# Attention and gated feed-forward on one core: a prologue with its weight casts, dummy matmuls and exps moved to other places and engines

## The chip, the cores and the metric

The kernel runs on one core of one Trainium2 chip. The time is the device time of one execution in microseconds (us); lower is better. The span in the profile is about 1.8 us shorter than that time. The granted clock is the share of full speed that the records show for TensorE; here it is 1.0 or 0.5, and its mean over the span is given. Five engines work side by side, each through its own queue of instructions in the order of the program: TensorE (PE in the profile), VectorE (DVE), ScalarE (ACT), GpSimd (POOL) and SyncE (SP), which here issues all DMAs.

## The reference, cut to what matters

```python
# attention, per batch b (8) and head h (8); seq 576, head_dim 64
q_s = softmax(q, axis=-1)                  # over head_dim
k_s = softmax(k, axis=2)                   # over the sequence
kv  = einsum('bhsd,bhse->bhde', k_s, v)
x   = einsum('bhsd,bhde->bhse', q_s, kv)   # -> [4608 tokens, 512]
# feed-forward
h   = (x @ w1) * (x @ w2) @ w3             # w1, w2: 512x1024, w3: 1024x1024
out = h @ w_out                            # 1024x512
```

Inputs and the output are float32. The kernel casts to float16 on the chip and computes `W3O = w3 @ w_out` once, so that the feed-forward is two large steps: `s1` (both products with x, multiplied) and `s2` (times `W3O`).

## The kernel before

There are nine chunks of 512 tokens. Chunk j runs eight groups of `s1(j)` with the four groups of `s2(j-1)` between them, the attention "pieces" of batch j+1 and the elementwise work of batch j+2. This steady part comes after a prologue: attention of batch 0, `s1(0)`, the product `W3O`, `s2(0)`, attention of batch 1. The order in which the source issues instructions is the order in each engine's queue (`manual_schedule`).

```python
    def norm_q(b, i, eng):                 # eng is always nc.gpsimd (POOL)
        nc.vector.reciprocal(...)
        eng.tensor_tensor(out=eqn, in0=eqs, in1=dr, op=ALU.mult)
    ...
    def w3_t(ft):                          # cast a row block of w3, transpose it
        w316 = attn.tile([P, Fd], F16, tag="w316", name="w316", bufs=2)
        nc.gpsimd.tensor_copy(out=w316, in_=w32[("3", ft)])      # POOL
        ... eight transposes on PE, then a copy on DVE (w3T)
    def w3_m(ft):
        ... eight matmuls w3T x wosb, then nc.scalar.copy(out=W3O[ft], in_=wps)
    ...
    for fb in range(N_FT):
        s1(0, fb)
        ...
        if fb == 5:
            w3_t(0)
            for i in range(4):
                pcopy(out=wosb[i], in_=w32[("o", i)])            # POOL
        if fb == 6:
            w3_t(1)
    ...
    def elementwise_steps(b): ...          # ten steps: exp_q, sum_q, norm_q, exp_k, cast_v
    ew = elementwise_steps(1)
    for ft in range(N_FT):
        w3_m(ft)
        if ft + 2 < N_FT:
            w3_t(ft + 2)
        if ft == 4:
            ew[0](); ew[1](); ew[2]()      # ew[2] holds norm_q(1, 0): POOL
        if ft == 5: ...
    pc = pieces(1)
    s2(0, 0); pc[0](); s2(0, 1, alt=True); pc[1](); ...          # pieces of batch 1
    for f in elementwise_steps(2):         # all of batch 2's exps in one burst
        f()
    for j in range(1, N_CHUNK): ...        # pieces at steps 0, 1, 3, 5, 7 of twelve
```

`warm(n)` issues n dummy matmuls on a zero tile, to keep TensorE's clock up while real work waits.

The softmax here doesn't subtract the row's maximum and nothing guards it: scores larger than these inputs give would overflow.

Of the kernel before, what the change touches and what calls it, by code (L numbers as in the profile page):

```python
# [8 lines left out]
F32 = mybir.dt.float32  # L9
F16 = mybir.dt.float16  # L10
# [6 lines left out]
def kernel(  # L17
# [11 lines left out]
    nc = tc.nc  # L29
# [3 lines left out]
    P = 128  # L33
# [25 lines left out]
    def pAtt(shape, dtype):  # L59
        return psum.tile(shape, dtype, tag="att", name="att", bufs=2)  # L60

    def pAB():
        return psum.tile([P, CH], F32, tag="pab", name="pab", bufs=3)
# [10 lines left out]
    def load_qkv(b, which, i):  # L74
        src = {"q": q, "k": k, "v": v}[which]
        t = slot([P, 2, R * D])
        nc.sync.dma_start(  # L77
            out=t,
            in_=src[b, 4 * i:4 * i + 4].rearrange("(h g) (s r) d -> (g s) h (r d)", g=2, r=R))
        qkv32[(which, b, i)] = t  # L80
# [16 lines left out]
    def load_w3(ft):  # L97
        t = slot([P, Fd])
        nc.sync.dma_start(out=t, in_=moe_w3[ft * P:(ft + 1) * P, :])
        w32[("3", ft)] = t  # L100
# [4 lines left out]
    def exp_k(b, i, hh):  # L105
        if hh == 0:
            eks[(b, i)] = attn.tile([P, R, 2, D], F16, tag="ek", name="ek", bufs=4)
        nc.scalar.activation(  # L108
            out=eks[(b, i)][:, :, hh, :],
            in_=qkv32[("k", b, i)][:, hh].rearrange("p (r d) -> p r d", r=R), func=AF.Exp)  # L110
# [8 lines left out]
    def cast_v(b, i, copy, hhs=slice(0, 2)):  # L119
        copy(out=v16buf[b % 2][:, 2 * i:2 * i + 2, :, 0:D][:, hhs],  # L120
             in_=qkv32[("v", b, i)].rearrange("p h (r d) -> p h r d", r=R)[:, hhs])
# [21 lines left out]
    def piece_kv(b, i):  # L143
        kvp = pAtt([P, 2, 512], F32)
        for r in range(R):
            for g in range(2):
                rows = slice(64 * g, 64 * g + 64)
                nc.tensor.matmul(kvp[:, g, 0:130].rearrange("p (h e) -> p h e", h=2),  # L148
                                 lhsT=eks[(b, i)][rows, r].rearrange("p h d -> p (h d)"),
                                 rhs=v16buf[b % 2][rows, 2 * i:2 * i + 2, r, 0:65],  # L150
                                 start=(r == 0), stop=(r == R - 1))
        rc = attn.tile([P, 2], F32, tag="rc", name="rc", bufs=4)
        nc.vector.reciprocal(out=rc, in_=kvp[:, :, 64])
        kv2 = attn.tile([P, 2, D], F16, tag="kv2", name="kv2", bufs=4)
        for hh in range(2):
            sl = slice(64 * hh, 64 * hh + 64)
            nc.vector.tensor_tensor(
                out=kv2[sl], in0=kvp[sl, :, 65 * hh:65 * hh + 64],
                in1=rc[sl, :, None].broadcast_to([64, 2, 64]), op=ALU.mult)
        kvs[(b, i)] = kv2  # L160

    def piece_t(b, i):
        pt = pAtt([P, R, P], F16)
        for r in range(R):
            nc.tensor.transpose(pt[:, r, :], eqns[(b, i)][:, r].rearrange("p h d -> p (h d)"),  # L165
                                ident)
        qsT = attn.tile([P, 2, R, SP], F16, tag="qsT", name="qsT", bufs=3)
        nc.vector.tensor_copy(out=qsT.rearrange("p g r s -> p r g s"),  # L168
                              in_=pt.rearrange("p r (g s) -> p r g s", g=2))
        qsTs[(b, i)] = qsT.rearrange("p g r s -> p g (r s)")  # L170

    def piece_x(b, i, hf):
        xp = pAtt([P, 2, 512], F32)
        qsT, kv2 = qsTs[(b, i)], kvs[(b, i)]
        cols = slice(hf * HS, (hf + 1) * HS)
        for hh in range(2):
            rows = slice(64 * hh, 64 * hh + 64)
            for g in range(2):
                nc.tensor.matmul(xp[64 * g:64 * g + 64, hh, 0:HS], lhsT=kv2[rows, g, :],  # L179
                                 rhs=qsT[rows, g, cols], start=True, stop=True)  # L180
        nc.scalar.copy(out=xT[:, 2 * i:2 * i + 2, b * S + hf * HS:b * S + (hf + 1) * HS],  # L181
                       in_=xp[:, :, 0:HS])

    def pieces(b):
        return {0: lambda: piece_t(b, 0), 1: lambda: piece_t(b, 1),
                3: lambda: (piece_kv(b, 0), piece_kv(b, 1)),
                5: lambda: (piece_x(b, 0, 0), piece_x(b, 0, 1)),
                7: lambda: (piece_x(b, 1, 0), piece_x(b, 1, 1))}

    def warm(n):  # L190
        wp = pAtt([P, CH], F32)
        for _ in range(n):
            nc.tensor.matmul(wp, lhsT=zero[:, 0:P], rhs=zero, start=True, stop=True)

# [33 lines left out]

    w3Ts = {}

    def w3_t(ft):
        w316 = attn.tile([P, Fd], F16, tag="w316", name="w316", bufs=2)
        nc.gpsimd.tensor_copy(out=w316, in_=w32[("3", ft)])
        tp = pAtt([P, N_FT, P], F16)
        for gt in range(N_FT):
            nc.tensor.transpose(tp[:, gt, :], w316[:, gt * P:(gt + 1) * P], ident)  # L236
        w3T = attn.tile([P, N_FT, P], F16, tag="w3T", name="w3T", bufs=2)
        nc.vector.tensor_copy(out=w3T, in_=tp)  # L238
        w3Ts[ft] = w3T

    def w3_m(ft):
        wps = pO() if ft % 2 else pAB()
        for gt in range(N_FT):
            nc.tensor.matmul(wps, lhsT=w3Ts[ft][:, gt, :], rhs=wosb[gt // 2][:, gt % 2, :],  # L244
                             start=(gt == 0), stop=(gt == N_FT - 1))
        nc.scalar.copy(out=W3O[ft], in_=wps)
# [17 lines left out]
    for t in v16buf:  # L264
        nc.gpsimd.memset(t[:, :, :, 64:65], 1.0 / SC)

    warm(18)
    for i in range(2):
        for hh in range(2):
            exp_q(0, i, hh)  # L270
# [9 lines left out]
        load_wo(i)  # L280
    piece_t(0, 0)
    cast_v(0, 0, vcopy)
    warm(4)
    piece_t(0, 1)
    piece_kv(0, 0)
    exp_k(0, 1, 0)
    exp_k(0, 1, 1)
    cast_v(0, 1, acopy, slice(1, 2))
    piece_x(0, 0, 0)
    piece_x(0, 0, 1)  # L290
    cast_v(0, 1, vcopy, slice(0, 1))
    piece_kv(0, 1)
    vcopy(out=w1sb[0], in_=w32[(0, 0)])
    acopy(out=w2sb[0], in_=w32[(1, 0)])
    piece_x(0, 1, 0)
    piece_x(0, 1, 1)

    def cast_w12(qt):
        vcopy(out=w1sb[qt], in_=w32[(0, qt)])
        acopy(out=w2sb[qt], in_=w32[(1, qt)])  # L300

    for fb in range(N_FT):
        s1(0, fb)
        if fb == 0:
            cast_w12(1)
        if fb == 2:
            cast_w12(2)
        if fb == 4:
            cast_w12(3)
        if fb == 5:  # L310
            w3_t(0)
            for i in range(4):
                pcopy(out=wosb[i], in_=w32[("o", i)])
        if fb == 6:
            w3_t(1)
    for ft in range(2, 8):
        load_w3(ft)
    for which, i in LOADS:
        load_qkv(1, which, i)
    for which, i in LOADS:  # L320
        load_qkv(2, which, i)

    def elementwise_steps(b):
        st = []
        for i in range(2):
            st += [lambda i=i: exp_q(b, i, 0),
                   lambda i=i: (sum_q(b, i, 0), exp_q(b, i, 1)),
                   lambda i=i: (sum_q(b, i, 1), norm_q(b, i, nc.gpsimd))]
        for i in range(2):
            st += [lambda i=i: exp_k(b, i, 0),  # L330
                   lambda i=i: (cast_v(b, i, pcopy), exp_k(b, i, 1))]
        return st

    ew = elementwise_steps(1)
    for ft in range(N_FT):
        w3_m(ft)
        if ft + 2 < N_FT:
            w3_t(ft + 2)
        if ft == 4:
            ew[0]()  # L340
            ew[1]()
            ew[2]()
        if ft == 5:
            ew[3]()
            ew[4]()
            ew[5]()
        if ft == 6:
            ew[6]()
            ew[7]()
        if ft == 7:  # L350
            ew[8]()
            ew[9]()
    pc = pieces(1)
    s2(0, 0)
    pc[0]()
    s2(0, 1, alt=True)
    pc[1]()
    s2(0, 2)
    pc[3]()
    s2(0, 3, alt=True)  # L360
    pc[5]()
    pc[7]()
    for which, i in LOADS:
        load_qkv(3, which, i)
    for f in elementwise_steps(2):
        f()

    seq = [("g", 0), ("g", 1), ("t", 0), ("g", 2), ("g", 3), ("t", 1),
           ("g", 4), ("g", 5), ("t", 2), ("g", 6), ("g", 7), ("t", 3)]
    for j in range(1, N_CHUNK):  # L370
        pc = pieces(j + 1) if j + 1 < B else {}
        ew = elementwise_steps(j + 2) if j + 2 < B else []
        ld = LOADS if j + 3 < B else []
        for n, (kind, x) in enumerate(seq):
            if kind == "g":
                s1(j, x)
            elif j > 1:
                s2(j - 1, x)
            if n in pc:
                pc[n]()  # L380
            if n < len(ew):
                ew[n]()
            if n >= 4 and n - 4 < len(ld):
                load_qkv(j + 3, *ld[n - 4])
    for tb in range(4):
        s2(N_CHUNK - 1, tb, alt=tb % 2)

# [29 lines left out]
```

## Time and profile before

| | before |
|---|---|
| time, median of 2 runs | 272.95 us |
| span of the profiled run | 271.1 us |
| PE busy | 246.7 us (91%) |
| mean granted clock of TensorE | 0.969 |
| first `s1` matmul of chunk 1, of chunk 2 | 74.5 us, 97.3 us |

The rows below are from the page of the kernel before: the span in 40 slices of 6.8 us, each digit the busy share in tenths. PEclk is the granted TensorE clock in tenths, DMA the busy share of the DMA engines.

```profile
PE   8579779669749999999999999999999999999983
PEclk9968979979998999999999999999999999999999
DMA  7999999941399903593498359411311113212235
```

From the thirteenth slice on (81 us) PE is full. All that can be won cheaply lies in the first twelve slices. DMA is full from the start to about 59 us: that is the reading of inputs and weights.

The timeline of PE in the kernel before, three of its lines: start, duration, operation, count, and in brackets how long PE sat idle before it and what ended that.

```profile
35.55 0.90 PE L236 MATMUL att<-ident,w_416 128*128 128x128 f16 x8 [3.17 <-POOL w_416 L233]
56.32 1.03 PE L236 MATMUL att<-ident,w_614 128*128 128x128 f16 x8 [4.15 <-POOL w_614 L233]
80.02 1.09 PE L165 MATMUL att<-ident,eqn 128*128 128x128 f16 x9 [3.21 <-POOL eqn L134]
```

PE waits three times for POOL by more than 3 us (two waits of 2.09 and 0.54 us in the first 12 us are left out): for the cast of w3 piece 1 (`w_416`), of w3 piece 7 (`w_614`), and for a normalised q of batch 2 (`eqn`). The timeline of POOL in the kernel before shows why the first two casts are late (the columns are the same):

```profile
26.77 1.04 POOL L233 CAST w_385<-st 128x1024 f16<-128x1024 f32 x1 [15.54 <-DMA st<-in_moe_w_dram]
29.43 1.35 POOL L313 CAST wo_83<-st 128x1024 f16<-128x1024 f32 x1 [1.63 <-DMA st<-in_moe_w_out_dram]
...
33.47 1.04 POOL L313 CAST wo_86<-st 128x1024 f16<-128x1024 f32 x1 [0.30 <-DMA st<-in_moe_w_out_dram]
34.45 1.04 POOL L233 CAST w_416<-st 128x1024 f16<-128x1024 f32 x1
...
53.16 2.12 POOL L134 TENSOR_TENSOR eqn<-eq,dr 128x1152 f16<-128x1152 f16 x1 [5.90 <-DMA st<-in_q_dram]
55.23 1.04 POOL L233 CAST w_614<-st 128x1024 f16<-128x1024 f32 x1
```

By the landing records of the trace, `w_416` landed at 28.02 us, before all of w_out (29.38 to 33.41), but is cast after it: POOL's queue holds four w_out casts first, and each of them starts within 0.1 us of its landing. `w_614` landed at 41.12 us and stands behind `eqn`. POOL had nothing to do from 47.3 to 53.2 us: it is not busy, it is blocked. (The trace puts the 5.90 us down to a DMA of q. The q piece of batch 1 had landed by 42.6 us; its exp started on ACT only at 50.5 us, behind the `W3O` copy of the same loop step, and the sum and reciprocal on DVE ended at 53.0 us.)

The table by windows for the kernel before, with windows laid on the stretches in which its clock records show half speed, and one of the steady part; the value after the engines is the granted clock:

```profile
15.25:22.08 6.83, 5.98 (x24) 1.92 (x21) 2.46 (x6) 3.65 (x5) 0.00 (x0) 0.50 1.09 348
35.73:39.14 3.41, 3.41 (x15) 1.57 (x13) 0.69 (x1) 0.58 (x1) 1.79 (x2) 0.50 1.03 408
56.21:59.62 3.41, 3.30 (x14) 1.74 (x15) 2.13 (x4) 0.00 (x0) 0.05 (x1) 0.50 0.33 122
80.10:83.52 3.42, 3.42 (x16) 1.77 (x17) 1.45 (x2) 1.50 (x4) 3.42 (x3) 0.50 1.05 402
100.00:150.00 50.00, 50.00 (x350) 24.20 (x349) 29.69 (x55) 24.35 (x42) 12.83 (x8) 1.00 0.61 185
```

After each of the three gaps TensorE runs at half clock for 3.41 us: about 1.7 us more is lost (an estimate, half of 3.41). A fourth stretch, 15-22 us, follows the thin attention work of batch 0.

### The profile page before, as it was taken

To read this page: it belongs to the slowest core of one execution; us is meant where nothing else is said; L and a number is where in the kernel's file an instruction comes from. 1 tells how busy PE (TensorE), PEld (TensorE's weight loads), DVE (VectorE), ACT (ScalarE), POOL (GpSimd) and SP (SyncE) were. 2 spreads that over 40 slices of the span, in tenths; PEclk is the share of its full clock that TensorE was granted. 3 is DMA by queue.
4 is the path that set the end of the run, shared out by engine and by line. 5 is a ranking of instruction groups with operands and counts; after the bars stand their busy time and mean duration, and the time that the engine had idled before them with its cause. 6 is when DMAs were issued, how large, how long until landed. Compare 5 with 4: busy or idle time off the path is not lost.

```text
span 271.1 us, 4141 instructions
## 1 busy us (share of the span) xinstructions
PE 246.7 (91%) x1574; PEld 116.7 (43%) x1574; DVE 132.3 (49%) x235; ACT 108.0 (40%) x182; POOL 62.8 (23%) x50
## 2 busy tenths in 40 slices
PE   8579779669749999999999999999999999999983
PEld 3234335334325455445444544544454444444431
DVE  2735523433466648636734863673553344444432
ACT  5464302514293773543473355347214322212200
POOL 1600654144055623410360342036000000000000
PEclk9968979979998999999999999999999999999999
DMA  7999999941399903593498359411311113212235
GB/s 250 383 348 377 396 404 394 390 178 38 89 290 393 386 11 104 145 335 98 126 293 263 80 135 323 143 41 39 77 41 39 39 41 73 45 39 63 55 76 117
DMA packets 25300, 48.51 MB, mean 179 GB/s; under 512 B 2240, under 2 KB 6336, under 8 KB 25280
## 3 DMA queue, kind: packets, MB, share of 16 engines
q1 hardware_dynamic: 25280, 48.24, 56.0%
q8 instruction: 12, 0.20, 0.3%
q14 instruction: 8, 0.07, 0.1%
HBM read 38.80 MB, written 9.44 MB: 178 GB/s over the span
## 4 chain that ended last, share of the span: by engine, by line
PE 72%; DMA 16%; ACT 3%; POOL 2%; DVE 2%; SPq 1%; issue 1%; POOLq 0%; DVEq 0%
PE po L220 21%; PE pab L203 21%; PE pab L209 20%; DMA st<-in_moe_w_dram 8%; DMA st<-in_q_dram 4%; DMA st<-in_moe_w_out_dram 4%; PE att L165 3%; PE att L220 3%; PE att L148 3%; PE att L179 2%; POOL eqn L134 2%; PE pab L244 1%; ACT xT L181 1%; DVE osb L223 1%; SPq L77 1%
## 5 line engine op out<-in xcount | busy, mean ns | idle before, releaser
L134 POOL TENSOR_TENSOR eqn<-eq,dr 128x1152 f16<-128x1152 f16 x16 | 33.9, 2121 | 100.3 <-DVE dr L132 87.3
L220 PEld LDWEIGHTS <-abT 128*128 128x128 f16 x288 | 27.4, 98 | 34.4 <-issue 3.1
L223 DVE TENSOR_SCALAR osb<-po 128x512 f32<-128x512 f32 x32 | 22.1, 692 | 32.0 <-PE po L220 31.4
L181 ACT CAST xT<-att 128x576 f16<-128x576 f32 x32 | 18.9, 642 | 21.6 <-PE att L179 21.6
L127 DVE TENSOR_REDUCE ds<-eq 128x9 f32<-128x576 f16 x32 | 23.1, 742 | 6.8 <-ACT eq L115 6.8
L115 ACT ACTIVATE eq<-st 128x576 f16<-128x576 f32 x32 | 21.2, 686 | 2.6 <-DMA st<-in_q_dram 2.6
L108 ACT ACTIVATE ek<-st 128x576 f16<-128x576 f32 x32 | 20.7, 686 | 3.1 <-DMA st<-in_k_dram 3.1
L203 PE MATMUL pab<-xT,w_0_75 128*128 128x512 f16 x72 | 21.2, 417 | 0.5 <-ACT xT L181 0.5
L209 PE MATMUL pab<-xT,w_0_79 128*128 128x512 f16 x72 | 19.8, 400 | 0.0
L203 PE MATMUL pab<-xT,w_3_78 128*128 128x512 f16 x72 | 19.4, 393 | 0.0
L209 PE MATMUL pab<-xT,w_3_82 128*128 128x512 f16 x72 | 19.1, 388 | 0.1
L203 PE MATMUL pab<-xT,w_2_77 128*128 128x512 f16 x72 | 18.5, 380 | 0.0
L203 PE MATMUL pab<-xT,w_1_76 128*128 128x512 f16 x72 | 18.5, 380 | 0.0
L209 PE MATMUL pab<-xT,w_2_81 128*128 128x512 f16 x72 | 18.5, 379 | 0.0
L209 PE MATMUL pab<-xT,w_1_80 128*128 128x512 f16 x72 | 18.5, 379 | 0.0
L165 PE MATMUL att<-ident,eqn 128*128 128x128 f16 x144 | 11.1, 224 | 5.8 <-POOL eqn L134 5.8
L165 PEld LDWEIGHTS <-eqn 128*128 128x128 f16 x144 | 9.5, 100 | 10.4 <-POOL eqn L134 7.3
L220 PE MATMUL po<-W3O_87,abT 128*128 128x512 f16 x32 | 12.2, 381 | 1.5 <-DVE osb L223 0.8
L238 DVE COPY w3T<-att 128x1024 f16<-128x1024 f16 x8 | 5.5, 690 | 15.0 <-PE att L236 15.0
L168 DVE COPY qsT<-att 128x1152 f16<-128x1152 f16 x16 | 12.0, 749 | 1.7 <-PE att L165 1.6
L220 PE MATMUL po<-W3O_91,abT 128*128 128x512 f16 x32 | 12.1, 379 | 0.0
L220 PE MATMUL po<-W3O_92,abT 128*128 128x512 f16 x32 | 12.1, 379 | 0.0
(288 smaller groups left out, 361.3 us busy)
## 6 DMA issues: line engine op xcount, KB each, us to landing
st<-in_q_dram SPq DMA_DIRECT2D x16, 576.0 KB, 5.1
st<-in_k_dram SPq DMA_DIRECT2D x16, 576.0 KB, 7.6
st<-in_v_dram SPq DMA_DIRECT2D x16, 576.0 KB, 7.6
out_dram<-osb SPq DMA_DIRECT2D x72, 128.0 KB, 2.4
st<-in_moe_w_dram SPq DMA_DIRECT2D x16, 512.0 KB, 10.4
st<-in_moe_w_out_dram SPq DMA_DIRECT2D x4, 512.0 KB, 10.9
```

Source lines behind the costliest of these rows:

```text
L108: nc.scalar.activation(out=eks[(b, i)][:, :, hh, :], in_=qkv32[("k", b, i)][:, hh].rearrange("p (r d) -> p r d", r=R), func=AF.Exp)
L115: nc.scalar.activation(out=eqs[(b, i)][:, :, hh, :], in_=qkv32[("q", b, i)][:, hh].rearrange("p (r d) -> p r d", r=R), func=AF.Exp)
L127: nc.vector.tensor_reduce(out=dss[(b, i)][:, :, hh], in_=eqs[(b, i)][:, :, hh, :], axis=AX.X, op=ALU.add)
L134: eng.tensor_tensor(out=eqn.rearrange("p r h d -> p (r h) d"), in0=eqs[(b, i)].rearrange("p r h d -> p (r h) d"), in1=dr[:, :, None].broad ...
L148: nc.tensor.matmul(kvp[:, g, 0:130].rearrange("p (h e) -> p h e", h=2), lhsT=eks[(b, i)][rows, r].rearrange("p h d -> p (h d)"), rhs=v16bu ...
L165: nc.tensor.transpose(pt[:, r, :], eqns[(b, i)][:, r].rearrange("p h d -> p (h d)"), ident)
L168: nc.vector.tensor_copy(out=qsT.rearrange("p g r s -> p r g s"), in_=pt.rearrange("p r (g s) -> p r g s", g=2))
L181: nc.scalar.copy(out=xT[:, 2 * i:2 * i + 2, b * S + hf * HS:b * S + (hf + 1) * HS], in_=xp[:, :, 0:HS])
L203: nc.tensor.matmul(pa, lhsT=w1sb[qt][:, ct, fo:fo + P], rhs=xT[:, ct, t0:t0 + CH], start=(ct == 0), stop=(ct == N_CT - 1))
L209: nc.tensor.matmul(pb, lhsT=w2sb[qt][:, ct, fo:fo + P], rhs=xT[:, ct, t0:t0 + CH], start=(ct == 0), stop=(ct == N_CT - 1))
L220: nc.tensor.matmul(po, lhsT=abT[(j, ft)][:, tb * P:(tb + 1) * P], rhs=W3O[ft], start=(ft == 0), stop=(ft == N_FT - 1))
L223: nc.vector.tensor_scalar(out=osb, in0=po, scalar1=ISC, scalar2=None, op0=ALU.mult)
```

## The change

Its intent: no cast on an engine that is blocked, casts in the order in which weights arrive, no cold clock, and the exps of batch 2 not in one burst. The core of the diff:

```diff
-        nc.scalar.copy(out=xT[...], in_=xp[:, :, 0:HS])
+        (copy or nc.scalar.copy)(out=xT[...], in_=xp[:, :, 0:HS])   # DVE for one of batch 0's copies
 ...
     def warm(n):
-        wp = pAtt([P, CH], F32)
+        wp = pAB()
 ...                                  # dummies: 18, 4 (22)  ->  26, 6, 3, 3, 2 (40)
+    def w3_c(ft):
+        w316s[ft] = attn.tile([P, Fd], F16, tag="w316", name="w316", bufs=3)
+        (nc.scalar.copy if ft % 2 else nc.vector.tensor_copy)(out=w316s[ft], in_=w32[("3", ft)])
     def w3_t(ft):
-        w316 = attn.tile([P, Fd], F16, tag="w316", name="w316", bufs=2)
-        nc.gpsimd.tensor_copy(out=w316, in_=w32[("3", ft)])
+        w316 = w316s[ft]
 ...
         if fb == 5:
+            w3_c(0)
+        if fb == 6:
+            w3_c(1)
             w3_t(0)
-            for i in range(4):
-                pcopy(out=wosb[i], in_=w32[("o", i)])
-        if fb == 6:
-            w3_t(1)
+            vcopy(out=wosb[0], in_=w32[("o", 0)])
+            vcopy(out=wosb[1], in_=w32[("o", 1)])
+    w3_t(1)
+    vcopy(out=wosb[2], in_=w32[("o", 2)])
+    vcopy(out=wosb[3], in_=w32[("o", 3)])
+    w3_c(2)
 ...                                  # in the loop over ft:
         w3_m(ft)
+        if ft + 3 < N_FT:
+            w3_c(ft + 3)
         if ft + 2 < N_FT:
             w3_t(ft + 2)
 ...                                  # exps of batch 2 between the groups of s2(0):
     s2(0, 1, alt=True)
-    pc[1]()
+    ew[0]()
+    ew[1]()
+    pc[2]()
+    ew[2]()
     s2(0, 2)
 ...
-    for f in elementwise_steps(2):
-        f()
 ...                                  # chunk 1: pieces of batch 2, exps of batch 3
-            if n in pc:
+        pcs = dict(zip((3, 4, 6, 8, 10) if j == 1 else (0, 1, 3, 5, 7), pieces(j + 1) ...))
+            ews.setdefault(min(n + 3, 11) if j == 1 else n, []).append(f)
```

The loads of w3 and of batches 1 and 2 are also written earlier in the source, but their order on SP's queue is the same. Not shown either: the exps of batch 1 are dealt out differently over the w3 loop, batch 1's first piece stands before `s2(0, 0)`, and in the steady part each load is issued one step later.

More of the change, by code (lines that the diff above doesn't have):

```diff
@@ L170, in piece_t, with piece_x @@
         qsTs[(b, i)] = qsT.rearrange("p g r s -> p g (r s)")
-    def piece_x(b, i, hf):
+    def piece_x(b, i, hf, copy=None):
         xp = pAtt([P, 2, 512], F32)
@@ L180, in piece_x @@
                                  rhs=qsT[rows, g, cols], start=True, stop=True)
-        nc.scalar.copy(out=xT[:, 2 * i:2 * i + 2, b * S + hf * HS:b * S + (hf + 1) * HS],
-                       in_=xp[:, :, 0:HS])
+        (copy or nc.scalar.copy)(
+            out=xT[:, 2 * i:2 * i + 2, b * S + hf * HS:b * S + (hf + 1) * HS],
+            in_=xp[:, :, 0:HS])
     def pieces(b):
-        return {0: lambda: piece_t(b, 0), 1: lambda: piece_t(b, 1),
-                3: lambda: (piece_kv(b, 0), piece_kv(b, 1)),
-                5: lambda: (piece_x(b, 0, 0), piece_x(b, 0, 1)),
-                7: lambda: (piece_x(b, 1, 0), piece_x(b, 1, 1))}
+        return [lambda: piece_t(b, 0), lambda: piece_t(b, 1),
+                lambda: (piece_kv(b, 0), piece_kv(b, 1)),
+                lambda: (piece_x(b, 0, 0), piece_x(b, 0, 1)),
+                lambda: (piece_x(b, 1, 0), piece_x(b, 1, 1))]
     def warm(n):
-        wp = pAtt([P, CH], F32)
+        wp = pAB()
         for _ in range(n):
@@ L229 @@
     w3Ts = {}
+    w316s = {}
+    def w3_c(ft):
+        w316s[ft] = attn.tile([P, Fd], F16, tag="w316", name="w316", bufs=3)
+        (nc.scalar.copy if ft % 2 else nc.vector.tensor_copy)(out=w316s[ft], in_=w32[("3", ft)])
     def w3_t(ft):
-        w316 = attn.tile([P, Fd], F16, tag="w316", name="w316", bufs=2)
-        nc.gpsimd.tensor_copy(out=w316, in_=w32[("3", ft)])
+        w316 = w316s[ft]
         tp = pAtt([P, N_FT, P], F16)
@@ L265 @@
         nc.gpsimd.memset(t[:, :, :, 64:65], 1.0 / SC)
-    warm(18)
+    warm(26)
     for i in range(2):
@@ L282 @@
     cast_v(0, 0, vcopy)
-    warm(4)
+    warm(6)
     piece_t(0, 1)
     piece_kv(0, 0)
+    warm(3)
     exp_k(0, 1, 0)
@@ L291 @@
     cast_v(0, 1, vcopy, slice(0, 1))
+    warm(3)
     piece_kv(0, 1)
+    warm(2)
     vcopy(out=w1sb[0], in_=w32[(0, 0)])
@@ L295 @@
     piece_x(0, 1, 0)
-    piece_x(0, 1, 1)
+    piece_x(0, 1, 1, vcopy)
     def cast_w12(qt):
@@ L300, in cast_w12 @@
         acopy(out=w2sb[qt], in_=w32[(1, qt)])
+    for ft in range(2, 8):
+        load_w3(ft)
+    for which, i in LOADS:
+        load_qkv(1, which, i)
+    for which, i in LOADS:
+        load_qkv(2, which, i)
     for fb in range(N_FT):
@@ L310 @@
         if fb == 5:
+            w3_c(0)
+        if fb == 6:
+            w3_c(1)
             w3_t(0)
-            for i in range(4):
-                pcopy(out=wosb[i], in_=w32[("o", i)])
-        if fb == 6:
-            w3_t(1)
-    for ft in range(2, 8):
-        load_w3(ft)
-    for which, i in LOADS:
-        load_qkv(1, which, i)
-    for which, i in LOADS:
-        load_qkv(2, which, i)
+            vcopy(out=wosb[0], in_=w32[("o", 0)])
[4 more added lines that the diff above has]
+    w3_c(2)
     def elementwise_steps(b):
@@ L334 @@
     ew = elementwise_steps(1)
+    pc = pieces(1)
     for ft in range(N_FT):
         w3_m(ft)
+        if ft + 3 < N_FT:
+            w3_c(ft + 3)
         if ft + 2 < N_FT:
             w3_t(ft + 2)
-        if ft == 4:
-            ew[0]()
-            ew[1]()
-            ew[2]()
-        if ft == 5:
-            ew[3]()
-            ew[4]()
-            ew[5]()
-        if ft == 6:
-            ew[6]()
-            ew[7]()
-        if ft == 7:
-            ew[8]()
-            ew[9]()
-    pc = pieces(1)
+        for f in {4: ew[0:2], 5: ew[2:5], 6: ew[5:8], 7: ew[8:9]}.get(ft, []):
+            f()
+    pc[0]()
+    ew[9]()
+    ew = elementwise_steps(2)
     s2(0, 0)
-    pc[0]()
+    pc[1]()
     s2(0, 1, alt=True)
-    pc[1]()
+    ew[0]()
+    ew[1]()
+    pc[2]()
+    ew[2]()
     s2(0, 2)
+    ew[3]()
     pc[3]()
+    ew[4]()
     s2(0, 3, alt=True)
-    pc[5]()
-    pc[7]()
+    pc[4]()
+    ew[5]()
+    ew[6]()
+    ew[7]()
     for which, i in LOADS:
         load_qkv(3, which, i)
-    for f in elementwise_steps(2):
-        f()
     seq = [("g", 0), ("g", 1), ("t", 0), ("g", 2), ("g", 3), ("t", 1),
@@ L370 @@
     for j in range(1, N_CHUNK):
-        pc = pieces(j + 1) if j + 1 < B else {}
-        ew = elementwise_steps(j + 2) if j + 2 < B else []
+        pcs = dict(zip((3, 4, 6, 8, 10) if j == 1 else (0, 1, 3, 5, 7),
+                       pieces(j + 1) if j + 1 < B else []))
+        steps = elementwise_steps(j + 2) if j + 2 < B else []
+        ews = {}
+        for n, f in enumerate(steps):
+            ews.setdefault(min(n + 3, 11) if j == 1 else n, []).append(f)
+        if j == 1:
+            ews[0] = ew[8:9]
+            ews[1] = ew[9:10]
         ld = LOADS if j + 3 < B else []
@@ L378 @@
                 s2(j - 1, x)
-            if n in pc:
-                pc[n]()
-            if n < len(ew):
-                ew[n]()
-            if n >= 4 and n - 4 < len(ld):
-                load_qkv(j + 3, *ld[n - 4])
+            if n in pcs:
+                pcs[n]()
+            for f in ews.get(n, []):
+                f()
+            if n >= 5 and n - 5 < len(ld):
+                load_qkv(j + 3, *ld[n - 5])
     for tb in range(4):
```

## The prediction

> **What bounds it now.** From about 84 us to the end (271.1 us span) TensorE never stops: the engine table by windows gives 50.0 of 50 us busy at clock 1.00 in 100-150, 150-200 and 200-250, and the chain of waits there is matmuls only. The change leaves the order of that part alone, so nothing is to be had there. Before 84 us the chain runs through DMA, POOL and ACT. From the timeline of PE:
> - gap 32.4-35.6 us (3.2): transpose of w3 piece 1 waits for a POOL cast, which stands in POOL's queue behind four w_out casts that wait for landings (29.4-33.4 us);
> - gap 52.2-56.3 us (4.2): w3 piece 7 landed at 41.1 us, but its POOL cast stands behind the normalisation (eqn, 2.12 us) of batch 1;
> - gap 76.8-80.0 us (3.2): piece_t(2) waits for ACT's eight exps of batch 2 in a burst, then sums, then POOL eqn;
> - after each of the three the granted clock is 0.5 for 3.41 us, about 1.7-1.9 us lost each, and 0.5 in 15.3-22.1 us (about 2.6 us). The Trainium skill, "TensorE: Matmul & The Clock Gate", Part 1, names a window of about 3.4 us; the trace agrees;
> - small waits: xT copies, W3O copy to s2 (0.7).
>
> The input DMA is saturated (about 390 GB/s) from 0 to 59 us; the order of loads does not change, so landings stay: w_out 29.4-33.4, w3 up to 41.1, q of batch 1 42.6 and 44.1, batch 2 51.6-59.0 us.
>
> **What the change does.** Casts: DVE 0.69 us and ACT 1.05 us instead of POOL 1.04 us; the count of work is the same, and both engines are under 60% busy in 24-60 us. Added: 16 dummy matmuls, about 0.22 us each, all in gaps (small cost if any). One xT copy goes to DVE: s1 starts its second half about 0.5 us sooner.
>
> **Walking the new order by hand with these durations:** s1 of chunk 0 runs warm from 17.7 to about 31.6 us (41 before minus w3 work). Then w3_m(0) cannot end before w_out piece 3 has landed (33.4) and been cast: about 35.5 us. So most of what the extra dummies gain (2.6 us) is lost again in waiting for w_out; worth perhaps 0.7 us. Then w3_t/w3_m run at PE's pace (0.45 + 1.73 us per piece) and end at about 50.5 us, against 61.9. The eqn of batch 1 is ready about 50.5 and 52.6 us: just in time. s2(0) with the pieces of batch 1 (10.2 us) ends about 60.7; s1(1) starts about 61.3 us, against 74.5: 13.2 us won. In chunk 1 the 3.2 us gap and its 1.9 us cold stretch go: 5 us more, 18.4 us in all. I take off 1 us for a probable new cold window after the stall at 32-35 us (half a chance of 1.7), and 1 us for waits that I overlooked (qkv3 landing close to its exp; eqn just in time).
>
> **Prediction:** 256.5 us, 8 in 10 between 252.8 and 261.5. Faster by over 2%: 0.97; within 2%: 0.02; slower: 0.01.
>
> **Right if:** no PE wait for a POOL cast of w3; PE gaps before 80 us sum to under 5 us; the first s1 matmul of chunk 1 near 61-63 us, of chunk 2 near 79-81 (97.3 before); steady part still about 23.9 us per chunk; DMA landings unchanged; clock 1.00 from 15 to 22 us.
> **Wrong if:** the clock falls to half in 15-22 us still, or in several windows of the w3 stage; ACT, now with casts, W3O copies and exps in one queue, delays exps so that eqn comes late; a DVE or ACT cast that waits for a landing holds up evictions behind it; loads are issued late because slots free later.

## The result, and the profile after

| | before | after |
|---|---|---|
| time, median of 2 runs | 272.95 us | 257.1 us |
| span of the profiled run | 271.1 us | 255.1 us |
| PE busy | 246.7 us (91%) | 243.5 us (95%) |
| mean granted clock | 0.969 | 1.0 |
| first `s1` matmul of chunk 1 | 74.5 us | 63.0 us |
| first `s1` matmul of chunk 2 | 97.3 us | 80.4 us |
| chunk 2, first matmul to that of chunk 3 | 23.93 us | 24.72 us |

The ratio is 0.9419 (95% interval 0.9374 to 0.9465). Later the changed kernel had medians of 256.93 and 257.15 us against 273.44 and 272.83.

The same rows of the page of the changed kernel (slices of 6.4 us), then its windows at the places where the kernel before was cold:

```profile
PE   8999989897999999999999999999999999999982
PEclk9999999999999999999999999999999999999999
DMA  7999999994999219932991497211211321132135
```

```profile
15.25:22.08 6.83, 6.29 (x33) 2.43 (x32) 4.12 (x8) 4.17 (x6) 0.00 (x0) 1.00 1.09 349
35.73:39.14 3.41, 3.41 (x26) 1.88 (x24) 2.08 (x3) 1.63 (x2) 0.00 (x0) 1.00 1.02 407
100.00:150.00 50.00, 50.00 (x344) 23.89 (x343) 29.28 (x54) 24.88 (x44) 13.10 (x9) 1.00 0.62 201
```

The clock is never halved, and PE is full from the eleventh slice on (64 us). In 35.73-39.14 us PE does 26 matmuls and transposes where it did 15. The waits of PE in the changed kernel, first 90 us, longest in total first (waiter and releaser, us in total, times, longest):

```profile
PE pab L194 <- DVE zero L268: 1.2, 1, 1.2
PE pab L250 <- DVE wo_85 L334: 1.0, 1, 1.0
PE pab L204 <- ACT xT L181: 0.8, 2, 0.6
PE att L165 <- POOL eqn L134: 0.8, 1, 0.8
```

The cast of w3 piece 1 in the timeline of ACT in the changed kernel (the piece landed at 27.85 us):

```profile
29.05 1.05 ACT L236 CAST w_458<-st 128x1024 f16<-128x1024 f32 x1
```

No wait of over 1.2 us is left, and none for a cast of w3 on POOL. The 16.0 us of span come in two parts: 11.5 us up to the start of chunk 1, and 5.4 us inside chunk 1, less 0.8 us that chunk 2 gives back.

### The profile page after: what moved, and what is told of

Read it like the earlier page. It is cut to its first block, busy times and chain, and to the rows that moved or that the text cites. A ratio compares the mean times of both kernels' runs of the same rounds, so it can differ in the third digit from the quotient of the medians.

```text
span 255.1 us, 4178 instructions
## 1 busy us (share of the span) xinstructions
PE 243.5 (95%) x1592; PEld 115.6 (45%) x1592; DVE 137.4 (54%) x244; ACT 112.0 (44%) x185; POOL 50.2 (20%) x38
## 4 chain that ended last, share of the span: by engine, by line
PE 87%; DMA 4%; DVE 3%; ACT 2%; issue 1%; POOL 1%; DVEq 0%; POOLq 0%; ACTq 0%
PE pab L204 23%; PE pab L210 23%; PE po L221 22%; PE pab L194 4%; DMA st<-in_moe_w_dram 4%; PE att L148 3%; PE att L165 3%; PE att L221 3%; PE att L179 2%; PE pab L250 1%; PE po L250 1%; DVE osb L224 1%; POOL eqn L134 1%; PE att L242 1%; ACT xT L181 1%
## 5 line engine op out<-in xcount | busy, mean ns | idle before, releaser
L181 ACT CAST xT<-att 128x576 f16<-128x576 f32 x31 | 18.4, 641 | 18.8 <-PE att L179 18.7
L204 PE MATMUL pab<-xT,w_0_75 128*128 128x512 f16 x72 | 19.0, 379 | 1.3 <-ACT xT L181 0.8
L204 PE MATMUL pab<-xT,w_2_77 128*128 128x512 f16 x72 | 18.5, 380 | 0.0
L204 PE MATMUL pab<-xT,w_1_76 128*128 128x512 f16 x72 | 18.5, 380 | 0.0
L204 PE MATMUL pab<-xT,w_3_78 128*128 128x512 f16 x72 | 18.5, 379 | 0.0
L210 PE MATMUL pab<-xT,w_3_82 128*128 128x512 f16 x72 | 18.5, 379 | 0.0
L210 PE MATMUL pab<-xT,w_1_80 128*128 128x512 f16 x72 | 18.5, 379 | 0.0
L210 PE MATMUL pab<-xT,w_2_81 128*128 128x512 f16 x72 | 18.5, 379 | 0.0
L210 PE MATMUL pab<-xT,w_0_79 128*128 128x512 f16 x72 | 18.5, 379 | 0.0
L194 PE MATMUL pab<-zero 128*128 128x512 f16 x40 | 12.0, 454 | 1.2 <-DVE zero L268 1.2
L221 PE MATMUL po<-W3O_87,abT 128*128 128x512 f16 x32 | 12.2, 381 | 0.8 <-DVE osb L224 0.8
L221 PE MATMUL po<-W3O_91,abT 128*128 128x512 f16 x32 | 12.1, 379 | 0.0
L221 PE MATMUL po<-W3O_92,abT 128*128 128x512 f16 x32 | 12.1, 379 | 0.0
L221 PE MATMUL po<-W3O_93,abT 128*128 128x512 f16 x32 | 12.1, 379 | 0.0
L221 PE MATMUL po<-W3O_94,abT 128*128 128x512 f16 x32 | 12.1, 379 | 0.0
```

Source lines behind the costliest of these rows:

```text
L181: (copy or nc.scalar.copy)(out=xT[:, 2 * i:2 * i + 2, b * S + hf * HS:b * S + (hf + 1) * HS], in_=xp[:, :, 0:HS])
L194: nc.tensor.matmul(wp, lhsT=zero[:, 0:P], rhs=zero, start=True, stop=True)
L204: nc.tensor.matmul(pa, lhsT=w1sb[qt][:, ct, fo:fo + P], rhs=xT[:, ct, t0:t0 + CH], start=(ct == 0), stop=(ct == N_CT - 1))
L210: nc.tensor.matmul(pb, lhsT=w2sb[qt][:, ct, fo:fo + P], rhs=xT[:, ct, t0:t0 + CH], start=(ct == 0), stop=(ct == N_CT - 1))
L221: nc.tensor.matmul(po, lhsT=abT[(j, ft)][:, tb * P:(tb + 1) * P], rhs=W3O[ft], start=(ft == 0), stop=(ft == N_FT - 1))
```

## The experiments

My theory: what was won is the place of a few instructions in in-order queues (of the casts about 11 us, of the exps about 4.5), not the engine that they run on. The rivals: POOL was too slow for casts, so the engines count; or the dummy matmuls hold the clock up and that carries most of the gain. Each kernel below gave a correct result, and was timed in five rounds beside the kernel before.

### The changed kernel again

> The changed kernel itself, for comparison in the same rounds: 257.1 us, within 0.8; clock 1.00 from about 6 us to the end in its profile, wherever the phase of the clock's window falls.

Median 256.93 us (256.81 to 257.15). The next two runs, and the burst further down, are compared with it.

### The dummies as they were

```diff
-    warm(26)
+    warm(18)
-    warm(6)
+    warm(4)
-    warm(3)   # and the other two calls
-        wp = pAB()
+        wp = pAtt([P, CH], F32)
```

> The changed kernel with the dummy matmuls as they were before (18 and 4). Theory (w_out's landing at 33.3 us hides most of what they win): half clock again from about 15 to 19-22 us, s1 of chunk 0 ends near 34.0 instead of 31.9 us, the first w3 matmul group ends near 36.2 instead of 34.9 us, so the whole is 1.3 us longer, between 0.5 and 1.7. Rival A (what the cold stretch cost is lost in full): 2.6 us longer. Rival B (the dummies are what keeps the clock up all through the prologue): half clock in several later windows, 4 us or more longer.

Measured: 257.80 us, 0.87 us longer. One of the six runs took 259.0 us at a mean clock of 0.981, against 0.992 or 0.993 in the others. The window on the half-clock stretch of this run's profile:

```profile
16.36:19.77 3.41, 3.28 (x13) 0.93 (x8) 1.29 (x2) 2.00 (x4) 0.00 (x0) 0.50 1.09 348
```

Half clock came back there and nowhere later in that profile, so rival B falls, and with 0.87 us rival A too. The size is the theory's, but not its mechanism. I had said that the wait for w_out's landing would absorb the rest. In this profile and in that of the changed kernel's run just above, PE waits the same 0.96 us for the cast of w_out piece 2; that wait moved along with PE. What shrank were small waits: for the first w1 cast and an xT copy just before and in the first `s1` group (0.53 to 0.13 us), and for w3 piece 2 (0.30 us to nothing).

The timeline of DVE in the changed kernel shows why the w_out wait moves along:

```profile
29.51 0.69 DVE L213 TENSOR_TENSOR abT<-pab,a_449 128x512 f16<-128x512 f32 x1 [0.43 <-PE pab L210]
30.12 0.68 DVE L244 COPY w3T<-att 128x1024 f16<-128x1024 f16 x1
30.71 0.68 DVE L331 CAST wo_83<-st 128x1024 f16<-128x1024 f32 x1
31.31 0.69 DVE L332 CAST wo_84<-st 128x1024 f16<-128x1024 f32 x1
31.91 0.68 DVE L213 TENSOR_TENSOR abT<-pab,a_478 128x512 f16<-128x512 f32 x1
32.52 0.68 DVE L244 COPY w3T<-att 128x1024 f16<-128x1024 f16 x1
33.11 0.68 DVE L334 CAST wo_85<-st 128x1024 f16<-128x1024 f32 x1
```

DVE works without a pause here. `wo_85` landed at 31.93 us and waits for nothing but its turn, and its turn depends on `s1`'s last product, so on PE. A landing would have shown as an idle time in brackets.

### The casts back on POOL, in their new places

```diff
-        (nc.scalar.copy if ft % 2 else nc.vector.tensor_copy)(out=w316s[ft], ...)
+        nc.gpsimd.tensor_copy(out=w316s[ft], ...)
-            vcopy(out=wosb[0], ...)        # all four
+            pcopy(out=wosb[0], ...)
```

> The changed kernel with the casts of w3 and w_out back on POOL, but in the changed kernel's places of the program. Theory (what counts is the order in the queue, not the engine): 0.3 us longer, between -0.3 and 1.0; no PE wait over 1.5 us for POOL. Rival (the engine counts: POOL is too slow or too busy): the 3 and 4 us gaps and the cold windows come back, 8 us or more longer.

Measured: 257.05 us, 0.12 us longer. The waits of PE for POOL in this run's first 90 us:

```profile
PE att L242 <- POOL w L236: 0.7, 1, 0.7
PE att L165 <- POOL eqn L134: 0.6, 1, 0.6
...
PE pab L250 <- POOL wo L335: 0.3, 1, 0.3
```

The engine is not what counts. A cast takes 1.04 us on POOL, 0.68 us on DVE and 1.05 us on ACT, but POOL has the time, and it never holds a later landing in front of an earlier one any more.

### Only two casts moved, in the kernel before

```diff
         if fb == 5:
             w3_t(0)
+            w3_c(1)                       # w3 piece 1's cast ahead of w_out's
             for i in range(4):
                 pcopy(out=wosb[i], ...)
...
         if ft == 4:
+            w3_c(7)                       # piece 7's cast ahead of norm_q
             ew[0]()
```

Here `w3_c` is the old POOL cast, and `w3_t` no longer casts what is cast already.

> The kernel before with two casts moved in POOL's queue and nothing else: w3 piece 1 ahead of the four w_out casts, w3 piece 7 ahead of batch 1's normalisation. All casts stay on POOL, the old dummies stay. Theory (order in the queue): the 3.2 and 4.2 us gaps and both cold windows after them go, the half-clock stretch at 15-22 us and the gap in chunk 1 stay; about 10.4 us shorter than before, between 9 and 11.5. Rival (the engine and the dummies are needed too): under 5 us shorter.

Measured: 262.03 us against 273.30 us for the kernel before, 11.3 us shorter, ratio 0.960 (0.956 to 0.964). Two casts moved ahead in one queue give over two thirds of the gain. The longest wait of PE left after 20 us:

```profile
PE att L165 <- POOL eqn L134: 3.2, 1, 3.2
```

That is the third gap, which this kernel was not to cure. The half clock at 15-22 us stayed too.

### Only the engines changed, in the kernel before

```diff
     def w3_t(ft):
-        nc.gpsimd.tensor_copy(out=w316, in_=w32[("3", ft)])
+        (nc.scalar.copy if ft % 2 else nc.vector.tensor_copy)(out=w316, ...)
...
-                pcopy(out=wosb[i], ...)
+                vcopy(out=wosb[i], ...)
```

> The kernel before with its casts of w3 and w_out put on VectorE and ScalarE as in the change, but left at their old places of the program. Theory (the place counts): the w_out casts now block DVE until their landings, and each odd w3 piece's ACT cast stands behind the W3O copy of the group just before it, so PE waits about 1.6 us before pieces 3, 5 and 7; the first and last gap shrink; about 4.7 us shorter than before, between 2 and 7. Rival (the engines count): about 10 us shorter, as in the run that only reordered POOL's queue (11.3).

Measured: 269.85 us (267.13 to 270.16) against 272.83, 3.0 us shorter, ratio 0.988 (0.983 to 0.993). The waits of PE for casts:

```profile
PE att L236 <- ACT w L233: 5.6, 4, 1.6
PE att L236 <- DVE w L233: 1.5, 1, 1.5
```

Three of ACT's four are 1.62 us each, before pieces 3, 5 and 7: the cast stands behind the copy of `W3O` that the same loop step issued, and that copy waits for the matmuls. So other engines in the old places give about a quarter of what the place alone gives. I had expected 4.7 us, between 2 and 7.

### The dummies alone, in the kernel before

```diff
-    warm(18)
+    warm(26)          # and 6, 3, 3, 2 in pAB, as in the change
```

> The kernel before with the dummies of the changed kernel (26, 6, 3, 3, 2, in the other PSUM buffers) and nothing else. Theory: s1 runs at full clock from 17 us, but PE then waits longer for the POOL cast of w3 piece 1, whose end the landings of w_out set: no change, within 0.6 us; the gap grows from 3.2 to 4.5-6 us. Rival (the clock in 15-22 us is worth its 2.6 us by itself): 2 us or more shorter.

Measured: 274.21 us against 273.30, ratio 1.0046 (1.000 to 1.009): no gain, perhaps slightly longer, a little outside my 0.6 us. The timeline of POOL and the waits of PE in this run:

```profile
34.48 1.04 POOL L316 CAST wo<-st 128x1024 f16<-128x1024 f32 x1 [0.32 <-DMA st<-in_moe_w_out_dram]
35.47 2.03 POOL L233 CAST w<-st 128x1024 f16<-128x1024 f32 x2
```

```profile
PE att L236 <- POOL w L233: 10.2, 3, 5.3
```

PE reaches the same POOL cast sooner and waits 5.34 us for it instead of 3.17. In the profiled run the half clock after it lasted 6.83 us instead of 3.41. Here a faster stage in front of a blocked queue only made the wait longer.

### Batch 2's exps in one burst again, pieces at the old places

```diff
-    ew[0]() ... ew[7]()                   # between the groups of s2(0)
+    for f in elementwise_steps(2):
+        f()
-        pcs = dict(zip((3, 4, 6, 8, 10) if j == 1 else (0, 1, 3, 5, 7), ...
+        pcs = dict(zip((0, 1, 3, 5, 7), ...
-            ews.setdefault(min(n + 3, 11) if j == 1 else n, []).append(f)
+            ews.setdefault(n, []).append(f)
```

> The changed kernel with batch 2's exps in one burst after s2(0) and its pieces at the old places of chunk 1. Theory: a PE gap of about 3 us in chunk 1 for POOL eqn and a cold window after it come back, less the 0.8 us that the late piece costs chunk 2: 4.4 us longer, between 3 and 5.5. Rival (with batch 1 earlier there is slack and the burst no longer hurts): under 1.5 us longer.

Measured: 261.35 us, 4.4 us longer. The longest waits of PE for POOL after 20 us in this run:

```profile
PE att L165 <- POOL eqn L134: 4.1, 2, 3.2
```

The third gap is back. This run also weighs a cold stretch: five of the six runs took 261.3 to 261.6 us at a clock of 0.988 to 0.993; the sixth took 259.66 us at a clock of 1.000. The difference is 1.7 us, half of 3.41.

### The burst with the late pieces, and the spread exps with the early pieces

These two take apart what the change did for batch 2. In the first the exps are in one burst as above, and the pieces stay late:

> The changed kernel with batch 2's exps in one burst after s2(0), but its pieces late as changed. Theory: PE no longer waits for eqn, but ACT's burst of eight exps (about 5 us) stands before the first a16 copy of chunk 1, and with three PSUM buffers PE stops after some 2.6 us: 2.4 us longer than the changed kernel, between 1.5 and 4. Rival: the place of the pieces is what counts; under 0.8 us longer.

Measured: 261.53 us, 4.6 us longer than the changed kernel's 256.93 us. It was run on another chip. PE's longest wait after 20 us, and ACT at that time:

```profile
PE pab L210 <- ACT a L207: 2.7, 1, 2.7
```

```profile
63.75 2.40 ACT L115 ACTIVATE eq<-st 128x576 f16<-128x576 f32 x4
66.06 2.39 ACT L108 ACTIVATE ek<-st 128x576 f16<-128x576 f32 x4
68.35 1.05 ACT L207 CAST a<-pab 128x512 f16<-128x512 f32 x2
```

The wait for `eqn` is gone as expected, and a new one of 2.74 us has come in its place: the copy that empties `s1`'s result buffer (`pab`) stands behind eight exps. The 4.6 us lie outside my range: I had expected 2.4 us, between 1.5 and 4, and left out a cold stretch after the gap; this profile has one, 3.41 us from 69.96 us, which by the same estimate accounts for 1.7 of the 2.2 us that I was short.

In the second the exps are spread, and the pieces go back to their old places:

> The changed kernel with batch 2's exps spread as changed, but its pieces at the old places of chunk 1 (after s1 groups 0, 1, ...). Theory: with the exps done early, eqn of batch 2 is ready in time, so the later places of the pieces are not needed, and the 0.6 us wait for an xT copy at the start of chunk 2 goes: 0.6 us shorter than the changed kernel, between 0.0 and 0.9. Rival: the pieces had to be later; the POOL gap comes back, 2 us or more longer.

Measured: median 256.19 us (255.88 to 259.14, seven runs), 0.7 us shorter than that 256.93 us; against the kernel before the ratios are 0.9385 and 0.9387, so this run by itself doesn't settle so small a difference. It was run on another chip. What its profile does show: chunk 2 takes 23.93 us again instead of 24.72, as the wait of 0.6 us for an xT copy at its start is gone. So the late places were not needed, and they are where the 0.8 us in chunk 2 were lost. Of the four combinations of exps and pieces, the two with spread exps are the fast ones, whatever the pieces: the exps' place does the work.

The one run of 259.14 us was the profiled one, and shows what else can happen. The timeline of PE, and the window on the stretch that follows:

```profile
34.56 0.59 PE L250 MATMUL pab<-wo,w3T 128*128 128x512 f16 x2 [1.20 <-DVE wo L334]
35.47 0.59 PE L250 MATMUL pab<-wo,w3T 128*128 128x512 f16 x2 [0.31 <-DVE wo L335]
36.74 0.71 PE L242 MATMUL att<-ident,w 128*128 128x128 f16 x8 [0.68 <-DVE w L236]
```

```profile
37.14:40.55 3.41, 3.41 (x12) 1.31 (x10) 1.38 (x2) 1.05 (x1) 0.00 (x0) 0.50 1.03 401
```

Gaps of 1.20, 0.31 and 0.68 us within 3.4 us were followed by a cold window. This part of the program is the same in the changed kernel, whose profile shows 0.97 and 0.29 us there and no cold window. The prediction had named this risk.

### The two placements together, in the kernel before

The two POOL casts moved, and batch 2's exps spread; casts on POOL, old dummies, old places of the pieces.

> The kernel before with the two casts moved ahead in POOL's queue and batch 2's exps spread over s2(0) and chunk 1, nothing else: casts on POOL, old dummies, pieces at their old places. Theory: the two moves in the queues are nearly the whole of the gain; 262.0 less the 3.2 us gap and 1.7 us of cold clock is 257.1 us, between 256.3 and 258.3, no more than 1 us from the changed kernel. Rival (without dummies and engines some of it is lost): above 259.

Measured: 257.45 us against 257.15 us for the changed kernel:

> The changed kernel once more, for comparison in the same rounds: 256.9 us, within 0.8.

The two placements alone come within 0.3 us of the whole change, although the half clock at 15-22 us is still there. The clock row of this run's page (slices of 6.4 us):

```profile
PEclk9967999999999999999999999999999999999998
```

All else in the change (engines, dummies, the copy moved to DVE, late pieces, the places of batch 1's exps and first piece) nets to about nothing. It isn't nothing part by part: without the new dummies the changed kernel lost 0.87 us, and its late pieces cost it 0.8 us in chunk 2 by the profiles, so these two nearly cancel. The DVE copy of xT and the moves within batch 1 were not tried alone.

### A better version

```diff
-        for f in {4: ew[0:2], 5: ew[2:5], 6: ew[5:8], 7: ew[8:9]}.get(ft, []):
+        for f in {3: ew[0:2], 4: ew[2:5], 5: ew[5:7], 6: ew[7:8], 7: ew[8:9]}.get(ft, []):
-            vcopy(out=wosb[0], ...)        # all four
+            pcopy(out=wosb[0], ...)
-        pcs = dict(zip((3, 4, 6, 8, 10) if j == 1 else (0, 1, 3, 5, 7), ...
+        pcs = dict(zip((0, 1, 3, 5, 7), ...
```

> The changed kernel with batch 2's pieces at their old places (0.7 us in the run of that alone), batch 1's exps one w3 group earlier so that eqn is ready (PE waited 0.8 us), and w_out's casts on POOL, which is idle there, so that they do not stand behind DVE's other work (PE waited 1.0 and 0.3 us; I expect 0.4 to 0.8 of it back). About 255.0 us, between 254.4 and 255.9, 1.9 us shorter than the changed kernel. Rival (the waits hide one another): no better than 256.2.

Measured: 255.53 us (255.35 to 255.85) against 257.15 us (256.86 to 257.99): 1.6 us shorter, and all of its six runs are faster than all six of the changed kernel. Its ratio to the kernel before is 0.937, that of the changed kernel 0.943. The two largest waits of PE that it has left after 20 us:

```profile
PE pab L250 <- POOL wo L335: 0.8, 1, 0.8
PE att L221 <- ACT xT L181: 0.6, 1, 0.6
```

The waits for `eqn` and at chunk 2 are gone. Of the w_out wait nothing was won, where I had expected 0.4 to 0.8 us: PE waits 0.21 and 0.76 us instead of 0.97. It is now the last w_out piece's landing and its 1.04 us on POOL that PE waits for, so there the landing does set the pace, as the prediction had it; in the changed kernel DVE's queue had made PE wait a little earlier, and for as long.

## Why the prediction was right

- **The total.** 256.5 us was predicted and 257.1 measured, inside the range. It was a sum of gaps and cold stretches read from the timeline before, and a walk through the new order with durations from the trace. That it came within 0.6 us is partly luck: the walk by itself gave 18.4 us, the parts measured 11.5 + 5.4 - 0.8 = 16.1, and of the 2 us taken off, 1 us was for a cold window that the profiled run did not have.
- **"Gap 32.4-35.6", "gap 52.2-56.3": casts behind others in POOL's queue.** Right: moving just these two casts gave 11.3 us. The Trainium skill, "TensorE: Matmul & The Clock Gate", Part 1, says in its paragraph on queue depths that ACT and DVE run their queues strictly first in, first out, and GPSIMD each of its Q7 cores; `w_416`, landed at 28.02 us, waited on POOL until 34.45 us behind casts of later loads, while in the changed kernel the same piece's cast, on ACT, started at 29.05 us, 1.2 us after the landing.
- **"Gap 76.8-80.0", the burst.** Right: with the burst back, 4.4 us came back. I put 5 us on it: 3.2 for the gap and 1.9 for the clock. The 0.8 us that the late pieces then cost chunk 2 were not foreseen.
- **"Clock 0.5 for 3.41 us" after each gap.** Right: the skill's window of about 3.4 us (same page and part) fits stretches of 3.41, 3.42 and 6.83 us (two of them) here, and one stretch was weighed at 1.7 us. The starts of the cold stretches in the kernel before, 15.25, 35.73, 56.21 and 80.10 us, lie 6, 6 and 7 times 3.41 us apart, so they begin on a grid of that step.
- **"Most of what the extra dummies gain is lost again in waiting for w_out; worth perhaps 0.7 us."** The size was right (0.87 us), the reason was not: PE's wait for w_out's piece 2 came from DVE's own queue and moved along with PE. (There are 18 more dummies, not 16 as the prediction counts; they lie in gaps either way.) I had treated DVE as an engine with time to spare because it was to be under 60% busy in 24-60 us; it was busy for 23.5 of these 36 us (65%), and from 29.5 to 34.4 us it had no pause at all.
- **"s1(1) starts about 61.3 us."** Measured 63.0. I summed `s2(0)` and the pieces to 10.2 us without their small waits (0.25, 0.62 and 0.53 us in the profile after), and `eqn` came 0.8 us late where I had "just in time". My 2 us of allowance covered it.
- **Landings unchanged, loads not late.** Right: each load of the weights and of batches 0 to 2 landed within 0.5 us of its time before (w3's last 40.98 against 41.12 us, batch 2's last 59.43 against 59.03).

## What to carry to other kernels

When an engine is idle and yet late, look at what stands in front of the late instruction in its queue, and issue work in the order in which its inputs arrive; here that was worth 11 us with no engine changed, while other engines in the old places gave 3 us. Before speeding up a stage, look at what the next stage waits for: here, dummies that kept the clock up won nothing by themselves, because the next cast was still blocked. A burst on an in-order engine moved its cost here rather than hid it (4.4 us longer with early pieces, 4.6 with late ones), so spread it in the slots where that engine is idle before the first consumer needs it.

## What the Trainium skill lacked or had wrong

- "TensorE: Matmul & The Clock Gate" gives as the rule against a cold clock that there be no idle gap of PE over about 3.4 us (section "HAM oscillation — how this bites in real kernels"), and in a later table over about 3 us. Single gaps of 3.17, 3.21 and 4.15 us here were followed by half clock, two of them under the first figure. But gaps of 1.20, 0.31 and 0.68 us close together were followed by 3.41 us at half clock too, and in the kernel before, small attention matmuls with gaps of 0.5 to 0.6 us between them by 6.83 us. So the rule is not enough. The page's next section does name short idles between groups of matmuls, but how busy a window must be I did not find there. On the grid of 3.41 us, the window before the cold one of the run with gaps of 1.20, 0.31 and 0.68 us has PE busy for 1.58 us; in the run with only the engines changed two windows with 1.79 and 1.80 us (gaps of 1.62 us) were not followed by half clock, but in the kernel before, 2.18 us of small matmuls were. So busy time alone does not settle it either.
- The same page says that the window runs free of the kernel. The runs agree: counted in steps of 3.41 us from the start of the span, the cold stretches begin at another part of a step in another run (15.25 us in the kernel before is 1.60 us into a step; 16.36 and 37.14 us in two other runs are 2.71 and 3.01 us into one). They give it a price too: with the same program, five runs of six at a clock of 0.988 to 0.993 took 261.3 to 261.6 us, and one at 1.000 took 259.66 us.
- No page that I read says that a low busy share hides a blocked queue: POOL was 23% busy over the span of the kernel before and DVE 54% over that of the changed one, and both held PE up by the order in their queues.
